# A three-stage attention and mixing kernel: cheaper softmax bookkeeping on VectorE, and the cast of x on ScalarE

## Chip, core and metric

One core of one Trainium2 chip runs the whole program. The metric is the device time of one execution in microseconds. The engines are named as in the profile: PE (TensorE matmul) and PEld (its weight load), DVE (VectorE), ACT (ScalarE), POOL (GpSimd) and SP (SyncE, which issues most of the DMAs).

## The reference, cut to what matters

Three functions follow one another, with batch 4, sequence 576 and model width 512.

```python
# 1: attention over a window of 64 keys, 8 heads of 64
scores = scale * q @ k.T;  scores = where(0 <= rel < 64, scores, -1e9)
attn = exp(scores - max);  attn /= sum(attn) + 1e-09;  x = attn @ v
# 2: four attention experts with a top-2 gate
logits = x @ w_gate;  w = exp(top2 - max);  w /= sum(w) + 1e-09
for e in range(4):                       # causal attention, q, k, v of expert e
    a = exp(scores - max);  a /= sum(a) + 1e-09
    out += [e is among the top 2] * w_e * (a @ v @ wo[e])
# 3: mixing
theta = x @ w_theta;  u = x + w_tok_r @ (x cos theta) + w_tok_i @ (x sin theta)
return u + max(u @ w_ch, 0)
```

## The kernel before, in words

Products that need more than one pass keep each operand as a high part and a low part (`h`, `l`), and `mm3` (L92 to L95) adds three matmuls. `split` (L84 to L90) makes such a pair: a cast for the high part on one engine, and a subtraction for the low part on another.

`phase_a` (L196 on) is function 1: for each of 4 batches and 4 pairs of heads it handles 9 blocks of 64 queries in 3 groups `g` of 3. The scores go to PSUM (L214), L219 masks them and takes the row minimum `nm` of the negated scores, L227 is the Exp with the sums in `sm`, L232 adds 1e-9, L233 takes the reciprocal `rc`, and POOL scales the tile (L234). Transposes (L239), the product with v (L249) and a split into `x0h`, `x0l` follow.

`qk` and `vg_gates` make q, k, v and the gates of function 2. L296 copies v and the logits out of PSUM; L305 to L331 compute the gate weights `gw` for all 576 tokens of a batch. L311 to L317 compare every logit with every other: two copies broadcast them (`lf`, `le`), then a greater-than, an equality, a product with the tie matrix and an addition.

`attn(b, ep)` handles two experts of one batch, in five steps `t` of 64 or 128 queries against the `w` keys up to them. For each expert `i` the scores come in one piece, or for t = 4 in two (`cuts`); L376 masks a piece and takes its minimum, L382 joins the two minima, L384 is the Exp with the sum. L388 adds 1e-9 for both experts, L389 takes the reciprocal, L390 multiplies it by the gate weight, and L392 to L400 scale P, part into `pd` and the rest in place; a table (`KN["SC"]`) says for each pass of `attn` which of these scalings are POOL's (through `pool_mul`, L82) and which are DVE's (L398). A scaling of POOL occurs in 29 of the 40 steps. Transposes (L409, L415), copies to `pT` and the product with v (L424, L428) follow; `wo` projects the result into `x2T`.

Function 3 starts with `x_split(b)`, which splits x in 4 pieces of 128x512 per batch, plus one piece `xt` for each pair of batches (the last 64 tokens of both): casts on DVE (L89, tiles `cx` and `xth`), subtractions on POOL (L90). `theta` makes the angles (L490, L492), sines and cosines on ACT (L493 to L495), products (L508, L517) and their splits (tile `z`). `mix` and `channel` are long runs of matmuls with weights that `load64` takes in from double precision; the last of these loads (`w64k`, `w64c`) are issued from ACT's queue, behind a late Exp of function 2 (L384).

The program's text interleaves these generators by weights (`merge`). The order in each engine's queue is then set when the program is built, by the framework's own simulation of the timeline (`schedule_with_timeline_sim=True` at the end of the file), so it need not be that of the text. Each engine works its queue in order; a wait at its head holds everything behind it.

Of the kernel before, what the change touches and what calls it, by code (L numbers as in the profile page):

```python
# [11 lines left out]
F32 = mybir.dt.float32  # L12
# [5 lines left out]
ALU = mybir.AluOpType  # L18
AX = mybir.AxisListType
PSUM = bass.MemoryType.PSUM  # L20

P = 128
# [35 lines left out]
def kernel(ctx, tc, qT, kT, vw, consts, w_in, w_o, w_th, w_tk, w_ch, outT):  # L58
    nc = tc.nc
# [6 lines left out]
    tie = cst[:, 4 * P :].rearrange("p (a b) -> p a b", a=E)  # L66
# [80 lines left out]


# [36 lines left out]
    def phase_a(b, hps):  # L185
        xh, xl = X[b]
        for hp in hps:
# [10 lines left out]
            for g in range(3):  # L198
# [26 lines left out]
                sm = ap.tile([P, 3], F32, tag="sm", bufs=4, name=f"asm{n}")  # L225
                for i in range(3):
                    nc.scalar.activation(  # L227
                        out=ms[:, i, :], in_=ms[:, i, :], func=AF.Exp,
                        bias=nm[:, i : i + 1], scale=-1.0, accum_out=sm[:, i : i + 1],
                    )  # L230
                rc = ap.tile([P, 3], F32, tag="rc", bufs=4, name=f"arc{n}")
                nc.vector.tensor_scalar_add(out=rc, in0=sm, scalar1=1e-9)  # L232
# [53 lines left out]
    def vg_gates(b):  # L286
# [22 lines left out]
        lf = bp.tile(sh4, F32, tag="glf", name=f"glf{b}")  # L309
        le = bp.tile(sh4, F32, tag="gle", name=f"gle{b}")  # L310
        nc.vector.tensor_copy(out=lf, in_=lg.unsqueeze(2).to_broadcast(sh4))  # L311
        nc.vector.tensor_copy(out=le, in_=lg.unsqueeze(3).to_broadcast(sh4))
        gt = bp.tile(sh4, F32, tag="ggt", name=f"ggt{b}")
        nc.vector.tensor_tensor(out=gt, in0=lf, in1=le, op=ALU.is_gt)
        nc.vector.tensor_tensor(out=le, in0=lf, in1=le, op=ALU.is_equal)
        nc.vector.tensor_mul(out=le, in0=le, in1=tie.unsqueeze(1).to_broadcast(sh4))
        nc.vector.tensor_add(out=gt, in0=gt, in1=le)  # L317
# [26 lines left out]
    def attn(b, ep):  # L344
# [7 lines left out]
        for t in range(5):  # L352
# [4 lines left out]
            if b == B - 1 and ep == 1 and t % 3 == 1:  # L357
                pn = rp.tile([P, 2, S], F32, tag="bmsx", name=f"bms{b}{ep}{t}")
            else:
                pn = bp.tile([P, 2, S], F32, tag="bms", bufs=2, name=f"bms{b}{ep}{t}")  # L360
            sm = bp.tile([P, 2], F32, tag="bsm", bufs=4, name=f"bsm{b}{ep}{t}")
            pd = bp.tile([P, 2, 64], F32, tag="bpd", bufs=2, name=f"bpd{b}{ep}{t}")
            for i in range(2):
# [6 lines left out]
                for ci, (a, z) in enumerate(cuts):  # L370
# [7 lines left out]
                        scale=-0.125, scalar=3.0e38, op0=ALU.add, op1=ALU.min,  # L378
                        accum_out=nm[:m, ci : ci + 1],
                    )  # L380
                if len(cuts) == 2:
                    nc.vector.tensor_tensor(out=nm[:m, 0:1], in0=nm[:m, 0:1],  # L382
                                            in1=nm[:m, 1:2], op=ALU.min)
                ex = nc.scalar.activation(out=ms[:m, :w], in_=ms[:m, :w], func=AF.Exp,  # L384
                                     bias=nm[:m, 0:1], scale=-1.0, accum_out=sm[:m, i : i + 1])
                if (b, ep, t, i) == (3, 1, KN["LT"], 1):
                    late[0] = ex
            nc.vector.tensor_scalar_add(out=sm[:m], in0=sm[:m], scalar1=1e-9)  # L388
            nc.vector.reciprocal(out=sm[:m], in_=sm[:m])  # L389
            nc.vector.tensor_mul(out=sm[:m], in0=sm[:m], in1=gw[:m, t, 2 * ep : 2 * ep + 2])  # L390
            for i in range(2):
                eng = nc.gpsimd if (False, i == 1 and t < 4, i == 1, t >= 2, i == 1 or t >= 3, True)[KN["SC"][2 * b + ep]] else nc.vector  # L392
                ms = pn[:, i]
                for dst, src in ((pd[:m, i], ms[:m, P * t : w]), (ms[:m, : P * t], ms[:m, : P * t])):
                    if src.shape[1] == 0:
                        continue
                    if eng is nc.vector:
                        eng.tensor_scalar_mul(out=dst, in0=src, scalar1=sm[:m, i : i + 1])  # L398
                    else:
                        pool_mul(dst, src, sm[:m, i : i + 1])  # L400
# [55 lines left out]
    def x_split(b):  # L456
        XH[b] = hl_set(xtags, f"cx{b}")
        for c in range(NC):
            split(XH[b][0][c][:, :W4], XH[b][1][c][:, :W4], x2T[b][:, c, :W4], nc.vector, nc.gpsimd)
        if b % 2 == 0:  # L460
# [5 lines left out]
            split(xth, xtl, xt, nc.vector, nc.gpsimd)  # L466
# [256 lines left out]
```

## Time and profile before

| | us |
|---|---|
| median of 3 runs | 546.76 (546.28 to 548.08) |
| the profiled execution: its own time | 546.72 |
| its span in the profile | 544.7 |
| busy in the span: PE, PEld | 518.1 (95%), 483.2 (89%) |
| busy in the span: DVE, ACT, POOL | 357.3 (66%), 323.7 (59%), 298.7 (55%) |

Times in views are counted from the start of the span. The profiled execution's own time is 2.0 us more than its span. Function 1 alone runs until some 58 us; functions 1 and 2 of different batches run side by side until some 320 us, and function 3 begins with its first casts at 276.6 us and runs to the end. Busy shares over the whole span mix stages with different limits, so the views below go by stage. A matmul's end is modelled in this profile: an instruction every 0.13 us is shown as 0.29 us long, so small gaps on PE don't show as idle time.

### The profile page before, as it was taken

The page shows a single profiled execution, that of the slowest core. Times are in us where ns is not written, and L with a number is a line of the kernel's source. Part 1 is how long each engine was busy: PE and PEld are TensorE (multiplying, and loading weights), DVE is VectorE, ACT ScalarE, POOL GpSimd, SP SyncE. Part 2 cuts the span into 40 slices and gives each one's busy share as a digit, 9 for nine tenths or more (in the row PEclk, how much of TensorE's full clock was granted, in tenths as well). Part 3 has the DMA queues.
Part 4 walks back from the last instruction along what each step waited for, and adds up shares of the span by engine and source line. Part 5 has one row for each costly group of instructions (what it writes and reads, how often), then busy time and mean ns, then how long its engine had stood idle before and what let it go on. Part 6 is the DMA issues. An engine that isn't in the chain of part 4 may idle for free.

```text
span 544.7 us, 12460 instructions
## 1 busy us (share of the span) xinstructions
PE 518.1 (95%) x4372; PEld 483.2 (89%) x4372; DVE 357.3 (66%) x1354; ACT 323.7 (59%) x1031; POOL 298.7 (55%) x455
## 2 busy tenths in 40 slices
PE   7879999999999999999799899799999999999997
PEld 5669978898888898989687799699999999999997
DVE  5886898857888688658989868863354435443412
ACT  6967687865868677878577887551344324432410
POOL 5686598635757662237764676962464415641420
PEclk8989999999999999999799899999999999999999
DMA  7654233322224231103003212001000110011002
GB/s 271 203 183 134 67 117 90 92 76 48 98 76 129 93 117 31 40 7 100 32 0 109 88 59 74 6 1 55 34 2 0 43 48 1 1 44 46 0 1 88
DMA packets 20798, 36.80 MB, mean 68 GB/s; under 512 B 2304, under 2 KB 13056, under 8 KB 20736
## 3 DMA queue, kind: packets, MB, share of 16 engines
q1 hardware_dynamic: 19008, 31.55, 18.5%
q10 hardware_dynamic: 1728, 4.46, 2.4%
q8 instruction: 35, 0.57, 0.5%
q14 instruction: 27, 0.22, 0.1%
HBM read 31.28 MB, written 4.72 MB: 66 GB/s over the span
## 4 chain that ended last, share of the span: by engine, by line
PE 69%; DVE 15%; ACT 4%; POOL 4%; DMA 4%; issue 3%; SPq 1%; ACTq 0%; POOLq 0%; DVEq 0%
PE y L94 6%; PE y L93 6%; PE y L95 6%; PE as L214 4%; PE c L94 3%; PE c L95 3%; PE c L93 3%; PE ao L249 3%; PE o L424 3%; PE th L93 3%; PE th L95 3%; PE th L94 3%; PE apt L239 2%; PE bpt L409 2%; PE qk L93 2%
## 5 line engine op out<-in xcount | busy, mean ns | idle before, releaser
L90 POOL TENSOR_TENSOR z<-zf,z 128x256 fp32r<-128x256 f32 x72 | 53.9, 765 | 88.3 <-ACT z L87 88.2
L93 PE MATMUL y<-wkh,z 128*128 128x288 f32 x288 | 86.1, 300 | 0.3 <-DVE x2T L541 0.3
L94 PE MATMUL y<-wkl,z 128*128 128x288 f32 x288 | 85.0, 296 | 0.0
L95 PE MATMUL y<-wkh,z 128*128 128x288 f32 x288 | 84.7, 297 | 0.0
L227 ACT ACTIVATE ams<-ams,anm 128x128 f32<-128x128 f32 x144 | 56.9, 398 | 8.0 <-DVE anm L219 6.5
L93 PEld LDWEIGHTS y<-wkh,z 128*128 128x128 f32 x288 | 54.1, 188 | 0.6 <-DVE x2T L541 0.6
L94 PEld LDWEIGHTS y<-wkl,z 128*128 128x128 f32 x288 | 54.2, 188 | 0.0
L95 PEld LDWEIGHTS y<-wkh,z 128*128 128x128 f32 x288 | 53.9, 188 | 0.0
L493 ACT ACTIVATE ang<-ang 128x256 f32<-128x256 f32 x36 | 14.6, 415 | 65.9 <-DVE ang L492 65.9
L384 ACT ACTIVATE bms<-bms,bnm 64x64 f32<-64x64 f32 (+4 forms) x80 | 44.7, 561 | 14.1 <-DVE bnm L376 7.0
L234 POOL TENSOR_TENSOR ams<-ams,arc 128x384 f32<-128x384 f32 x48 | 40.3, 842 | 23.1 <-DVE arc L233 11.4
L82 POOL TENSOR_SCALAR QD<-qt 64x192 f32<-64x192 f32 x72 | 39.6, 550 | 22.5 <-PE as L214 18.8
L87 ACT CAST z<-zf 128x256 fp32r<-128x256 f32 x72 | 27.3, 403 | 39.1 <-DVE zf L508 14.5
L214 PE MATMUL as<-kt,QD 128*128 128x128 f32 x288 | 45.5, 298 | 3.6 <-ACT QD L209 2.7
L214 PEld LDWEIGHTS as<-kt,QD 128*128 128x128 f32 x288 | 38.4, 203 | 7.8 <-ACT QD L209 3.1
L508 DVE TENSOR_TENSOR zf<-xk,ang 128x256 f32<-128x256 f32 x64 | 25.1, 419 | 28.1 <-ACT ang L495 17.9
L376 DVE CUSTOM_DVE_ANT_0 bms<-bs,mb 128x288 f32<-128x288 f32 (+4 forms) x96 | 38.8, 427 | 5.7 <-PE bs L374 3.1
L219 DVE CUSTOM_DVE_ANT_0 ams<-as,cst 128x128 f32<-128x128 f32 x144 | 34.5, 284 | 7.5 <-PE apt L239 5.0
L93 PE MATMUL th<-wth,cx 128*128 128x256 f32 x128 | 36.6, 287 | 0.5 <-DVE ang L492 0.5
L554 DVE SCALAR_TENSOR_TENSOR x2T<-c,x2T 128x288 f32<-128x288 f32 x32 | 14.5, 457 | 34.0 <-PE c L95 33.8
L94 PE MATMUL th<-wtl,cx 128*128 128x256 f32 x128 | 36.0, 282 | 0.0
L90 POOL TENSOR_TENSOR cu<-x2T,cu 128x288 fp32r<-128x288 f32 x32 | 26.1, 836 | 17.8 <-ACT cu L87 17.8
(196 smaller groups left out, 1752.2 us busy)
## 6 DMA issues: line engine op xcount, KB each, us to landing
vt<-in_dram SPq DMA_DIRECT2D x48, 192.0 KB, 2.4
kt<-in_dram SPq DMA_DIRECT2D x16, 320.0 KB, 3.4
qt<-in_dram SPq DMA_DIRECT2D x16, 288.0 KB, 3.2
out_dram<-x2T SPq DMA_DIRECT2D x32, 144.0 KB, 1.8
w64k<-in_dram SPq DMA_DIRECT2D x5, 576.0 KB, 3.8
w64k<-in_dram ACTq DMA_DIRECT2D x4, 576.0 KB, 3.8
w64t<-in_dram SPq DMA_DIRECT2D x4, 512.0 KB, 4.8
w64c<-in_dram ACTq DMA_DIRECT2D x8, 256.0 KB, 2.8
```

Source lines behind the costliest of these rows:

```text
L82: nc.gpsimd.tensor_scalar(out=out, in0=in_, scalar1=by, scalar2=1.0, op0=ALU.mult, op1=ALU.mult)
L87: nc.scalar.copy(out=dst_h, in_=src)
L90: eng_l.tensor_sub(out=dst_l, in0=src, in1=f32(dst_h))
L93: nc.tensor.matmul(out, wh, xh, start=first, stop=False)
L94: nc.tensor.matmul(out, wh, xl, start=False, stop=False)
L95: nc.tensor.matmul(out, wl, xh, start=False, stop=last)
L214: nc.tensor.matmul(s[:, i, :], QD[g][:, i], kt[:, 64 * blk : 64 * blk + 128], start=True, stop=True)
L219: nc.vector.tensor_tensor_reduce(out=ms[:, i, :], in0=s[:, i, :], in1=ma0 if (g == 0 and i == 0) else ma1, scale=-0.125, scalar=3.0e38, op ...
L227: nc.scalar.activation(out=ms[:, i, :], in_=ms[:, i, :], func=AF.Exp, bias=nm[:, i : i + 1], scale=-1.0, accum_out=sm[:, i : i + 1],)
L234: nc.gpsimd.tensor_mul(out=ms, in0=ms, in1=rc.unsqueeze(2).to_broadcast([P, 3, P]))
L376: nc.vector.tensor_tensor_reduce(out=ms[:m, a:z], in0=s[:m, : z - a], in1=mb[:m, mo + a : mo + z], scale=-0.125, scalar=3.0e38, op0=ALU.ad ...
L384: ex = nc.scalar.activation(out=ms[:m, :w], in_=ms[:m, :w], func=AF.Exp, bias=nm[:m, 0:1], scale=-1.0, accum_out=sm[:m, i : i + 1])
```

## The change

Five edits, and no other line differs.

1. The sums of the Exps go into column 0 of small tiles (`AS`, `BS`) whose column 1 holds 1e-9; 8 memsets write that once at the start, and the tiles are used in turn, four of each kind. In place of the addition of 1e-9 (L232, L388) a `tensor_reduce` adds the two columns.
2. In `x_split` the casts go from DVE to ACT.
3. The multiplication of the reciprocal by the gate weight (L390) is dropped; the scaling of P takes the gate weight as its second per-partition scalar, on DVE and on POOL.
4. The minimum of the first piece is the starting value of the second piece's minimum, and L382 is dropped.
5. In the gates the two copies are dropped: one subtraction of two broadcast views, then two `scalar_tensor_tensor`, for the former six instructions.

```diff
@@ -144,6 +144,17 @@
           tc.alloc_tile_pool(name="xp1", bufs=1, side="left")]
     xbuf = [[xp[i].tile([P, NC, S], F32R, name=f"x{i}{n}") for n in "hl"] for i in range(2)]
     ap = tc.alloc_tile_pool(name="ap", bufs=1, side="right")
+
+    AS = [ap.tile([P, 3, 2], F32, name=f"AS{i}") for i in range(4)]
+    BS = [bp.tile([P, 2, 2], F32, name=f"BS{i}") for i in range(4)]
+    for x in AS + BS:
+        nc.gpsimd.memset(x[:, :, 1], 1e-9)
+    nsum = [0, 0]
+
+    def sums(kind, tiles):
+        nsum[kind] += 1
+        return tiles[nsum[kind] % 4]
+
 
 
     QD = [ap.tile([P, 3, P], F32, name=f"QD{i}") for i in range(3)]
@@ -222,14 +233,14 @@
                         scale=-0.125, scalar=3.0e38, op0=ALU.add, op1=ALU.min,
                         accum_out=nm[:, i : i + 1],
                     )
-                sm = ap.tile([P, 3], F32, tag="sm", bufs=4, name=f"asm{n}")
+                sm = sums(0, AS)
                 for i in range(3):
                     nc.scalar.activation(
                         out=ms[:, i, :], in_=ms[:, i, :], func=AF.Exp,
-                        bias=nm[:, i : i + 1], scale=-1.0, accum_out=sm[:, i : i + 1],
+                        bias=nm[:, i : i + 1], scale=-1.0, accum_out=sm[:, i, 0:1],
                     )
                 rc = ap.tile([P, 3], F32, tag="rc", bufs=4, name=f"arc{n}")
-                nc.vector.tensor_scalar_add(out=rc, in0=sm, scalar1=1e-9)
+                nc.vector.tensor_reduce(out=rc, in_=sm, op=ALU.add, axis=AX.X)
                 nc.vector.reciprocal(out=rc, in_=rc)
                 nc.gpsimd.tensor_mul(
                     out=ms, in0=ms, in1=rc.unsqueeze(2).to_broadcast([P, 3, P])
@@ -306,15 +317,13 @@
         ex = bp.tile([P, 5, E], F32, tag="gex", name=f"gex{b}")
         nc.vector.tensor_sub(out=ex, in0=lg, in1=mx.unsqueeze(2).to_broadcast([P, 5, E]))
         nc.scalar.activation(out=ex, in_=ex, func=AF.Exp)
-        lf = bp.tile(sh4, F32, tag="glf", name=f"glf{b}")
-        le = bp.tile(sh4, F32, tag="gle", name=f"gle{b}")
-        nc.vector.tensor_copy(out=lf, in_=lg.unsqueeze(2).to_broadcast(sh4))
-        nc.vector.tensor_copy(out=le, in_=lg.unsqueeze(3).to_broadcast(sh4))
+        lf, lo = lg.unsqueeze(2).to_broadcast(sh4), lg.unsqueeze(3).to_broadcast(sh4)
+        df = bp.tile(sh4, F32, tag="gle", name=f"gdf{b}")
+        nc.vector.tensor_sub(out=df, in0=lf, in1=lo)
         gt = bp.tile(sh4, F32, tag="ggt", name=f"ggt{b}")
-        nc.vector.tensor_tensor(out=gt, in0=lf, in1=le, op=ALU.is_gt)
-        nc.vector.tensor_tensor(out=le, in0=lf, in1=le, op=ALU.is_equal)
-        nc.vector.tensor_mul(out=le, in0=le, in1=tie.unsqueeze(1).to_broadcast(sh4))
-        nc.vector.tensor_add(out=gt, in0=gt, in1=le)
+        nc.vector.scalar_tensor_tensor(out=gt, in0=df, scalar=0.0, in1=tie.unsqueeze(1).to_broadcast(sh4),
+                                       op0=ALU.is_equal, op1=ALU.mult)
+        nc.vector.scalar_tensor_tensor(out=gt, in0=df, scalar=0.0, in1=gt, op0=ALU.is_gt, op1=ALU.add)
         rk = bp.tile([P, 5, E], F32, tag="grk", name=f"grk{b}")
         nc.vector.tensor_reduce(out=rk, in_=gt, op=ALU.add, axis=AX.X)
         nc.vector.scalar_tensor_tensor(
@@ -358,6 +367,7 @@
                 pn = rp.tile([P, 2, S], F32, tag="bmsx", name=f"bms{b}{ep}{t}")
             else:
                 pn = bp.tile([P, 2, S], F32, tag="bms", bufs=2, name=f"bms{b}{ep}{t}")
+            ss = sums(1, BS)
             sm = bp.tile([P, 2], F32, tag="bsm", bufs=4, name=f"bsm{b}{ep}{t}")
             pd = bp.tile([P, 2, 64], F32, tag="bpd", bufs=2, name=f"bpd{b}{ep}{t}")
             for i in range(2):
@@ -375,29 +385,24 @@
                                      start=False, stop=True)
                     nc.vector.tensor_tensor_reduce(
                         out=ms[:m, a:z], in0=s[:m, : z - a], in1=mb[:m, mo + a : mo + z],
-                        scale=-0.125, scalar=3.0e38, op0=ALU.add, op1=ALU.min,
-                        accum_out=nm[:m, ci : ci + 1],
+                        scale=-0.125, scalar=nm[:m, 0:1] if ci else 3.0e38,
+                        op0=ALU.add, op1=ALU.min, accum_out=nm[:m, ci : ci + 1],
                     )
-                if len(cuts) == 2:
-                    nc.vector.tensor_tensor(out=nm[:m, 0:1], in0=nm[:m, 0:1],
-                                            in1=nm[:m, 1:2], op=ALU.min)
                 ex = nc.scalar.activation(out=ms[:m, :w], in_=ms[:m, :w], func=AF.Exp,
-                                     bias=nm[:m, 0:1], scale=-1.0, accum_out=sm[:m, i : i + 1])
+                                     bias=nm[:m, ci : ci + 1], scale=-1.0, accum_out=ss[:m, i, 0:1])
                 if (b, ep, t, i) == (3, 1, KN["LT"], 1):
                     late[0] = ex
-            nc.vector.tensor_scalar_add(out=sm[:m], in0=sm[:m], scalar1=1e-9)
+            nc.vector.tensor_reduce(out=sm[:m], in_=ss[:m], op=ALU.add, axis=AX.X)
             nc.vector.reciprocal(out=sm[:m], in_=sm[:m])
-            nc.vector.tensor_mul(out=sm[:m], in0=sm[:m], in1=gw[:m, t, 2 * ep : 2 * ep + 2])
             for i in range(2):
                 eng = nc.gpsimd if (False, i == 1 and t < 4, i == 1, t >= 2, i == 1 or t >= 3, True)[KN["SC"][2 * b + ep]] else nc.vector
                 ms = pn[:, i]
                 for dst, src in ((pd[:m, i], ms[:m, P * t : w]), (ms[:m, : P * t], ms[:m, : P * t])):
                     if src.shape[1] == 0:
                         continue
-                    if eng is nc.vector:
-                        eng.tensor_scalar_mul(out=dst, in0=src, scalar1=sm[:m, i : i + 1])
-                    else:
-                        pool_mul(dst, src, sm[:m, i : i + 1])
+                    eng.tensor_scalar(out=dst, in0=src, scalar1=sm[:m, i : i + 1],
+                                      scalar2=gw[:m, t, 2 * ep + i : 2 * ep + i + 1],
+                                      op0=ALU.mult, op1=ALU.mult)
             yield 0.25 * (t + 1)
             pT = bp.tile([P, 5, 2, P], F32, tag="bpT", bufs=2, name=f"bpT{b}{ep}{t}")
             for j0 in range(0, t, 2):
@@ -456,14 +461,14 @@
     def x_split(b):
         XH[b] = hl_set(xtags, f"cx{b}")
         for c in range(NC):
-            split(XH[b][0][c][:, :W4], XH[b][1][c][:, :W4], x2T[b][:, c, :W4], nc.vector, nc.gpsimd)
+            split(XH[b][0][c][:, :W4], XH[b][1][c][:, :W4], x2T[b][:, c, :W4], nc.scalar, nc.gpsimd)
         if b % 2 == 0:
             xt = kp.tile([P, NC, P], F32, tag="xt", name=f"xt{b}")
             for k in range(2):
                 pool_mul(xt[:, :, 64 * k : 64 * k + 64], x2T[b + k][:, :, W4:], 1.0)
             xth = kp.tile([P, NC, P], F32R, tag="xth", name=f"xth{b}")
             xtl = kp.tile([P, NC, P], F32R, tag="xtl", name=f"xtl{b}")
-            split(xth, xtl, xt, nc.vector, nc.gpsimd)
+            split(xth, xtl, xt, nc.scalar, nc.gpsimd)
             XT[0] = xt, xth, xtl
 
     def theta(b, dh):
```

## Rows read from the trace of the kernel before

**Rows 1.** Busy time by engine in stages of the run, with the column line.

```profile
core 0: us, PE busy (x) PEld busy (x) DVE busy (x) ACT busy (x) POOL busy (x), PEclk, DMA share, GB/s
0.00:58.00 58.00, 49.55 (x439) 42.79 (x440) 40.64 (x202) 42.86 (x159) 41.15 (x72) 0.94 0.61 195
58.00:260.00 202.00, 197.63 (x1859) 176.82 (x1857) 160.18 (x740) 151.27 (x529) 118.54 (x214) 1.00 0.26 79
260.00:320.00 60.00, 53.03 (x391) 46.91 (x390) 51.72 (x171) 43.39 (x119) 36.98 (x44) 0.91 0.15 50
320.00:360.00 40.00, 36.41 (x281) 35.41 (x281) 32.65 (x71) 24.30 (x69) 31.10 (x37) 1.00 0.12 41
360.00:540.00 180.00, 180.00 (x1400) 180.00 (x1399) 71.19 (x171) 61.92 (x157) 70.92 (x89) 1.00 0.08 26
```

**Rows 2.** The same columns as rows 1, in four stretches of 5 us.

```profile
260.00:265.00 5.00, 1.45 (x7) 1.16 (x6) 4.87 (x14) 3.25 (x10) 4.67 (x6) 0.78 0.01 6
265.00:270.00 5.00, 4.64 (x18) 4.19 (x17) 4.75 (x20) 3.11 (x7) 2.96 (x6) 0.54 0.00 0
300.00:305.00 5.00, 3.27 (x24) 2.44 (x23) 5.00 (x13) 2.63 (x7) 5.00 (x5) 0.88 0.59 200
345.00:350.00 5.00, 2.31 (x18) 2.11 (x17) 5.00 (x7) 1.06 (x3) 5.00 (x5) 1.00 0.00 0
```

**Rows 3.** Chain that ended last, shares by line: 260 to 280, 280 to 300 us.

```profile
by line: DVE bms L376 11.2%; DVE cx L89 10.3%; DVE gle L315 6.9%; DVE gsm L325 6.6%; PE qk L93 6.5%; DVE KL L282 6.4%; DVE gex L320 5.7%; DVE ggt L317 5.6%; PE qk L94 5.3%; PE qk L95 5.3%; DVE QS L279 4.7%; issue 4.2%; DVE ol L90 2.1%; PE b
...
by line: DVE bms L376 19.4%; issue 8.7%; DVE bsm L388 7.4%; DVE bpT L411 5.2%; DVE ol L90 4.6%; DVE bms L398 4.4%; ACT bms L384 4.4%; DVE bpd L398 4.2%; DVE KL L282 4.1%; PE o L424 4.0%; PE bs L372 4.0%; DVE bnm L382 3.6%; DVE xth L89 3.5%;
```

**Rows 4.** The same chain piece by piece, 340 to 360 us: start, us, what.

```profile
344.88 3.82 DVE cx L89 x3
348.69 0.66 DVE zf L508 x2
```

**Rows 5.** What PE waited for: us in total, times, longest.

```profile
PE xk L486 <- DVE zf L508: 2.7, 1, 2.7
```

**Rows 6.** DVE groups by line and shape: count, busy us, mean ns, idle before.

```profile
L232 DVE TENSOR_SCALAR arc<-asm 128x3 f32<-128x3 f32 x48 | 13.1, 272 | 8.0 <-ACT ams L227 7.6
...
L89 DVE CAST cx<-x2T 128x512 fp32r<-128x512 f32 x16 | 13.0, 846 | 0.1
...
L388 DVE TENSOR_SCALAR bsm<-bsm 128x2 f32<-128x2 f32 x32 | 10.1, 314 | 8.4 <-ACT bms L384 8.2
...
L390 DVE TENSOR_TENSOR bsm<-bsm,gw 128x2 f32<-128x2 f32 x32 | 7.2, 226 | 0.5
...
L382 DVE TENSOR_TENSOR bnm<-bnm 128x1 f32<-128x1 f32 x16 | 4.3, 270 | 0.2
...
L317 DVE TENSOR_TENSOR ggt<-ggt,gle 128x80 f32<-128x80 f32 x4 | 2.8, 690 | 0.1
...
L324 DVE TENSOR_REDUCE gsm<-gex 128x5 f32<-128x20 f32 x4 | 0.7, 171 | 0.1
...
L311 DVE COPY glf<-lg 128x80 f32<-128x80 f32 x4 | 0.9, 223 | 0.0
```

**Rows 7.** Two DVE lines by themselves: shortest/median/longest ns, first and last start.

```profile
L232 DVE TENSOR_SCALAR arc<-asm x48: 141/169/1296, 8.3 to 229.0; 128x3 f32<-128x3 f32 x48
...
L388 DVE TENSOR_SCALAR bsm<-bsm x40: 150/170/921, 61.1 to 305.3; 128x2 f32<-128x2 f32 x32, 64x2 f32<-64x2 f32 x8
```

**Rows 8.** An ACT group of the shape of the casts.

```profile
L130 ACT ACTIVATE wth<-wtut 128x512 fp32r<-128x512 f32 x4 | 2.5, 629 | 0.4 <-POOL wtut L122 0.4
```

**Rows 9.** ACT in order of time, 344 to 350 us.

```profile
349.12 0.71 ACT L87 CAST z<-zf 128x256 fp32r<-128x256 f32 x2 [3.77 <-DVE zf L508]
```

**Rows 10.** POOL groups by line and shape.

```profile
L82 POOL TENSOR_SCALAR bms<-bms,bsm 128x256 f32<-128x256 f32 x11 | 5.3, 487 | 0.6 <-ACT bpT L419 0.6
...
L82 POOL TENSOR_SCALAR xt<-x2T 128x256 f32<-128x256 f32 x4 | 1.6, 407 | 0.0
...
L70 POOL MEMSET halfpi<- 128x1 f32 x1 | 0.1, 99 | 0.0
```

## The prediction

> **What bounds the kernel now.** I read the stages first, since the five edits touch different ones [rows 1]. From 360 to 540 us PE and its weight loads are busy for all of 180 us, while DVE works 71 us: nothing that is taken off DVE there can pay. Before 360 us it is otherwise. PE shows 8.5 us of idle time up to 58 us (58.00 less 49.55), 4.4 us from 58 to 260, 7.0 us from 260 to 320 and 3.6 us from 320 to 360; 23 us in all are the room of this change, and small gaps that the modelled ends hide come on top. DVE is the busiest of the other engines in the last three of these stages, and from 260 to 320 us it has 51.72 of 60 us.
>
> Second, the worst stretches [rows 2]. From 260 to 265 us PE works 1.45 of 5 us and DVE 4.87; in the next 5 us the granted clock is 0.54, near 1.2 of 2.4 GHz, after that stall. From 300 to 305 and from 345 to 350 us DVE and POOL are both full and PE is not. There the queue of DVE sets the pace.
>
> Third, what of the chain in those stretches is a line that the change touches [rows 3]. From 260 to 280 us the casts `cx` take 10.3% of 20 us, 2.1 us, and the gate lines L315 and L317 6.9 and 5.6%, 2.5 us. From 280 to 300 us L388 takes 7.4%, 1.5 us, L382 3.6%, 0.7 us, and the cast of `xth` 3.5%, 0.7 us. Further on three casts hold DVE from 344.88 to 348.69 us, and the products `zf` follow only then [rows 4]; PE waits 2.7 us for them [rows 5].
>
> **The change part by part.** First what DVE is relieved of, in busy time.
>
> *Sums.* L232 takes 0.272 us on average, 48 times, and L388 0.314, 32 times and 8 at half the rows [rows 6]. Alone they would be as quick as their medians, 0.17 us; the longest are 1.30 and 0.92 us [rows 7]. No row shows a reduction of 2 or 3 pairs. The nearest is L324, 20 elements to 5, 0.171 us; its bounds here are 0.14, the shortest addition, and 0.27 to 0.31, the addition's own mean. I take 0.16, for it has fewer elements than L324 and no such stretched one stands in its mean. That is 48 x 0.11 = 5.3 us for L232 and 40 x 0.14 = 5.6 us for L388.
>
> The Trainium skill, "VectorE: DVE Perf Modes", section "Rules for kernel authors", speaks against this edit: it calls `tensor_reduce` the slowest operation of the engine and advises restructuring. By it these 10.9 us would not be won and the sum would be 540.9 instead of 539.2; L324's 0.171 us against L388's 0.314 speaks for the row.
>
> *Products and minima.* L390 goes, 32 x 0.226 us and 8 shorter ones, 8.3 us at most; L382 goes, 4.3 us [rows 6]. In L382's place the second piece of t = 4 waits for the first piece's accumulator. Behind that wait on DVE stand whatever evacuations the order has put there, and PE's next score bank waits for the second piece. Bounds: nothing, and L382's own 0.27 us, 16 times; I take nothing, since the wait is on the instruction directly before.
>
> *Gates.* Six groups, L311 first with 0.9 us and L317 last with 2.8 us, make 10.1 us in four batches [rows 6]. Three remain, of the same 80 elements and two inputs. Bounds for one are L311's 0.22 and L317's 0.69 us; I take 0.5, so 6 us remain and 4 us, 40%, go.
>
> *Casts.* 16 of 0.846 us [rows 6] and two `xth` leave DVE, some 15 us. ACT pays 18 x 0.63 = 11.3 us by L130, an ACT instruction of that shape [rows 8]. Ten of the 18 fall before 360 us, 6.3 us. ACT has 16.6 us free from 260 to 320 (60.00 less 43.39) and 15.7 from 320 to 360 [rows 1]; at the place of the three casts it sits idle for 3.77 us, waiting for DVE [rows 9], and three casts are 1.9 us. So I cost them at nothing; were that idle time filled, the 1.9 us would stand before the casts of `z`. ACT's queue also issues the last loads of weights, and a cast ahead of an issue makes that load 0.63 us later; PE has other matmuls in these stretches, so nothing, and 0.63 us for each where it has none. POOL's subtractions still follow each cast.
>
> The Trainium skill speaks against this edit too: by the cycle tables of "VectorE: DVE Perf Modes", section "The TRN2 errata", a 512-element fp32 copy is an estimated 0.33 us on VectorE and 0.61 on ScalarE. By them the three casts would be 1.0 us, which is all that could be won of the 2.7, and the five before 320 us 1.6 of the 2.8 below, 70% of it let through: the sum would be some 2.5 us less, 541.7. The trace has 0.846 us for a cast on DVE, and the trace decides.
>
> *Scaling.* With two per-partition scalars: no row shows it, on either engine. On POOL a 128x256 scaling by one such scalar takes 0.487 us, by none 0.407 [rows 10]; a second may cost nothing or 0.08 us more. In 29 of the 40 steps POOL scales, so the end is 2.3 us on the path if every step shows it; I take a third, 0.8. On DVE the bounds are nothing and the 0.16 us of L390's quick cases, which would cancel that edit; I take nothing, since the DVE instruction already fetches one scalar.
>
> *Memsets.* Eight at some 0.1 us, by L70 [rows 10], at the start on POOL, and read first by the reduction behind the first Exps, which wait for the loads: nothing; 0.8 us if they stand ahead of what PE waits for.
>
> **The sum**, by what reaches the end. From 320 to 360 us: the wait of 2.7 us [rows 5]. From 260 to 300: casts 2.8, gates 40% of 2.5 = 1.0, L388 1.5 less three reductions of 0.16 = 1.0, L382 0.7, 5.5 us together; what is late next is L376 and the copies to `pT` on the same engine, and PE, so I let 70% through, 3.8 us. From 58 to 260 us DVE saves some 20 us of 160 (three quarters of L388, L390, L382 and the gates, and most of L232), but PE has only 4.4 us of visible idle time; a third, 1.5 us. Up to 58 us L232 alone is touched, beside loads and POOL: 0.3 us. That is 8.3 us, less 0.8 for POOL: 7.5 us. From the profiled execution's 546.72 us this gives 539.2 us; its time stands 0.04 us below the median of the runs, so nothing is added.
>
> **The rivals.**
>
> *More than that.* If DVE no longer lags at the gates, the stall of 260 to 265 us goes whole, and with it the half clock behind it: 3.5 us of idle PE, and up to 2.3 us for the 5 us at 0.54 [rows 2], of which the sum holds some 2, so 3.8 more. With the other 30% of the 5.5 us, 1.7, and no price on POOL, 0.8, it makes 532.9 us. For it: DVE is full there. Against: POOL has 4.67 of those 5 us, and is relieved of nothing.
>
> *The bookkeeping saves nothing*, the change not doing what it says: the reductions stretch as the additions did, or DVE pays for the second scalar what L390 cost. The gain from 260 to 300 us falls by 0.7 to 1.5 us, the one before by 1 us: some 541.5 us. For it: the additions' spread [rows 7], whose cause may lie in their neighbours. Against: L324. The two rules of the Trainium skill named above lead near this case, at 540.9 and 541.7.
>
> *Swallowed.* PE's queue, ACT and POOL, at 43 and 37 of 60 us, are as late as DVE once it is quicker, and only the wait of rows 5 shrinks, by 1 us: 545.7 us. Against: DVE's part of the chain in rows 3.
>
> *Slower: the queues' new order.* The framework writes the order anew from its own costs; that it is not the text's is shown by casts of x at 276 us, ahead of L388 and L382 of attention steps still to come [rows 3]. The mechanism: at the hand-over to the next batch the gate sequence and the subtractions that release q and k stand in one DVE queue, and if the gates stand in front, PE stops. The price is shown at the fourth place, 258 to 270 us: 3.5 us idle and 2.3 us at half clock, some 6 us [rows 2]. The other three such places pay little, for the stage up to 260 has only 4.4 us of idle time in all. One more such place takes 6 of the 7.5 us back; it decides from two on: 539.2 + 12 = 551 us. For it: every edit alters the costs that the order is made from. Against: the three shorter gate instructions lower this price too.
>
> **How the numbers follow.** The forecast, 539.2 us with a range of its own of 535.5 to 543.5, has 0.40; more than that, 0.13; the bookkeeping saving nothing, 0.15; swallowed, 0.13; slower by the order, 0.19. About 0.3%, 1.6 us, is what a measurement of this kernel can tell from no change: faster ends at 545.1, slower begins at 548.4. Faster: 0.40 + 0.13 + 0.15 = 0.68; the same 0.13; slower 0.19. The range reaches down to 531.5, the last microsecond of the first rival left out, and up to 549.5, which takes in the swallowed case and the near end of the slower one.
>
> **What would show it.** Right: reductions of 0.15 to 0.18 us with no long ones; no casts on DVE, and ten on ACT near 0.63 us; `zf` right behind the x2T additions at some 345 us and PE's wait for it gone; DVE busy some 45 us less, ACT some 11 us more. Wrong: the stages up to 260 us longer than before with DVE emptier, which is the order; POOL's scalings above 0.57 us at 128x256; PE waiting for `cx` casts on ACT behind an Exp; or the wait of rows 5 standing as it was.

## The result, and the profile after

The changed kernel takes 540.72 us (median of four runs, 536.14 to 542.42), the one before, timed beside it, 546.52 (four runs, 545.85 to 548.08): 5.8 us less by the medians. The ratio with its 95% interval is 0.9875 [0.9847, 0.9903], 6.8 us less; it is not the quotient of the two medians, and here as in the experiments the two can differ by 1 us. The four runs of the changed kernel lie 6.3 us apart and those of the kernel before 2.2 us, and the profiled execution is the quickest of the four, 536.14 us, 4.6 us under the median. What its rows show beyond these 6 to 7 us belongs to that execution, not to the change.

The page of the kernel after: its span, the busy time of each engine, and the chain that ended last.

```profile
span 534.3 us, 12401 instructions
...
PE 511.4 (96%) x4372; PEld 479.2 (90%) x4372; DVE 326.4 (61%) x1268; ACT 331.2 (62%) x1049; POOL 303.9 (57%) x463
...
PE 76%; ACT 7%; DVE 6%; POOL 4%; DMA 3%; issue 3%; SPq 1%; ACTq 0%; POOLq 0%; DVEq 0%
```

DVE is busy for 30.9 us less than before, ACT for 7.5 and POOL for 5.2 us more. Some five times as much left DVE as left the run.

Busy time by stage of the kernel after, with the columns of [rows 1], and then the four stretches of 5 us of [rows 2], with the ones just ahead, 255 to 260 and 295 to 300 us:

```profile
58.00:260.00 202.00, 195.54 (x1842) 175.78 (x1842) 150.38 (x692) 151.91 (x533) 126.80 (x216) 1.00 0.27 79
260.00:320.00 60.00, 56.07 (x434) 50.71 (x433) 48.48 (x151) 47.99 (x130) 38.70 (x45) 0.94 0.17 58
320.00:360.00 40.00, 40.00 (x315) 39.80 (x315) 26.59 (x67) 26.83 (x75) 32.42 (x41) 1.00 0.09 27
...
255.00:260.00 5.00, 2.80 (x19) 2.31 (x18) 4.70 (x18) 3.41 (x12) 4.60 (x6) 1.00 0.34 115
260.00:265.00 5.00, 3.45 (x14) 2.87 (x13) 4.81 (x17) 1.54 (x4) 3.25 (x5) 0.53 0.02 3
265.00:270.00 5.00, 5.00 (x29) 4.71 (x28) 3.28 (x9) 3.90 (x11) 2.65 (x4) 0.79 0.00 0
...
295.00:300.00 5.00, 3.83 (x32) 3.05 (x32) 4.75 (x15) 4.92 (x13) 3.01 (x3) 1.00 0.52 161
300.00:305.00 5.00, 5.00 (x44) 4.52 (x45) 5.00 (x9) 5.00 (x13) 2.43 (x2) 1.00 0.20 80
345.00:350.00 5.00, 5.00 (x41) 5.00 (x40) 2.03 (x6) 1.35 (x4) 5.00 (x7) 1.00 0.02 3
```

Two of the stretches in which DVE had set the pace are full now, 300 to 305 and 345 to 350 us. Just ahead of the first, though, PE works 3.83 of 5 us from 295 to 300 us, where the kernel before had 4.59: a stall is left there, but the granted clock, 0.88 from 300 to 305 us before [rows 2], stays at 1.00. The stall at the fourth gates is not gone: it begins earlier, with 2.20 us of idle PE from 255 to 260 us and 1.55 in the next 5, and the granted clock falls again, to 0.53 from 260 to 265 us, near 1.2 of 2.4 GHz. Idle time and lost clock together make 3.75 us and (0.47 + 0.21) x 5 = 3.4 us from 255 to 270 us, 7.2 in all; before it was 3.9 us (3.55 and 0.36) and (0.22 + 0.46) x 5 = 3.4, 7.3 in all [rows 2]. This place gave nothing.

From 320 to 360 us PE waits for nothing, where the wait of [rows 5] stood. The place is seen best by two tiles. `y` starts with the first matmul of `mix`, `c` with the first of `channel`; from `c` on every kernel of this study needs 176.1 to 176.3 us to its end, so the distance from `y` to `c` measures that stage by itself. The view of each tile gives the shortest, median and longest ns and the first and last start; the kernel before, then the kernel after:

```profile
L93 PE MATMUL y<-wkh,z x288: 288/295/399, 321.7 to 528.2; 128*128 128x288 f32 x144
L93 PE MATMUL c<-cu,wch x64: 289/296/378, 368.5 to 540.1; 128*128 128x288 f32 x64
```

```profile
L93 PE MATMUL y<-wkh,z x288: 288/295/384, 315.3 to 517.8; 128*128 128x288 f32 x144
L93 PE MATMUL c<-cu,wch x64: 290/295/381, 358.0 to 529.7; 128*128 128x288 f32 x64
```

Before, 368.5 - 321.7 = 46.8 us; after, 358.0 - 315.3 = 42.7 us: 4.1 us of the gain lie here. The other 6.4 us of this profile lie ahead of `y`. The execution is 4.6 us quicker than the median run, and where the runs differ one profile cannot show.

The groups of the kernel after that answer to [rows 6] and [rows 8] (count, busy us, mean ns, idle before):

```profile
L243 DVE TENSOR_REDUCE arc<-AS 128x3 f32<-128x6 f32 x48 | 7.3, 152 | 8.9 <-ACT ams L238 8.6
...
L395 DVE TENSOR_REDUCE bsm<-BS 128x2 f32<-128x4 f32 x32 | 4.8, 151 | 5.3 <-ACT bms L391 5.2
...
L386 DVE CUSTOM_DVE_ANT_0 bms<-bs,mb,bnm 128x288 f32<-128x288 f32 x16 | 8.2, 511 | 1.2 <-PE bs L384 0.8
L386 DVE CUSTOM_DVE_ANT_0 bms<-bs,mb 128x288 f32<-128x288 f32 x16 | 7.1, 447 | 1.3 <-PE bs L384 1.0 <-PE bpt L414 0.2
...
L322 DVE TENSOR_TENSOR gdf<-lg 128x80 f32<-128x80 f32 x4 | 1.7, 432 | 0.0
L326 DVE SCALAR_TENSOR_TENSOR ggt<-gdf,ggt 128x80 f32<-128x80 f32 x4 | 1.5, 383 | 0.0
L324 DVE SCALAR_TENSOR_TENSOR ggt<-gdf,cst 128x80 f32<-128x80 f32 x4 | 1.2, 292 | 0.0
...
L87 ACT CAST cx<-x2T 128x512 fp32r<-128x512 f32 x16 | 9.5, 616 | 9.5 <-PE c L94 9.5
```

The reductions take 0.15 us, the three gate instructions 0.43, 0.29 and 0.38, a cast on ACT 0.616. Of the two pieces of 288 columns at t = 4, the second, which starts from the minimum of the first (`bnm` among its inputs), takes 0.064 us more; in the kernel before, where neither starts from a tile, the 32 of them take 0.448 us on average.

The price of the second scalar, by the view of one line: the kernel before on POOL and on DVE, then the kernel after (shortest, median, longest ns).

```profile
L82 POOL TENSOR_SCALAR bpd<-bms,bsm x47: 311/320/743, 68.1 to 301.4; 128x64 f32<-128x64 f32 x40, 64x64 f32<-64x64 f32 x7
...
L398 DVE TENSOR_SCALAR bpd<-bms,bsm x33: 238/251/1405, 87.2 to 306.8; 128x64 f32<-128x64 f32 x24, 64x64 f32<-64x64 f32 x9
```

```profile
L403 POOL TENSOR_SCALAR bpd<-bms,bsm,gw x47: 386/393/824, 62.9 to 292.7; 128x64 f32<-128x64 f32 x40, 64x64 f32<-64x64 f32 x7
...
L403 DVE TENSOR_SCALAR bpd<-bms,bsm,gw x33: 297/307/1210, 82.8 to 302.7; 128x64 f32<-128x64 f32 x24, 64x64 f32<-64x64 f32 x9
```

By the shortest it is 0.075 us on POOL (386 - 311) and 0.059 on DVE (297 - 238).

### The profile page after: what moved, and what is told of

Read it like the earlier page. It is cut to its first block, busy times and chain, and to the rows that moved or that the text cites. A ratio compares the mean times of both kernels' runs of the same rounds, so it can differ in the third digit from the quotient of the medians.

```text
span 534.3 us, 12401 instructions
## 1 busy us (share of the span) xinstructions
PE 511.4 (96%) x4372; PEld 479.2 (90%) x4372; DVE 326.4 (61%) x1268; ACT 331.2 (62%) x1049; POOL 303.9 (57%) x463
## 4 chain that ended last, share of the span: by engine, by line
PE 76%; ACT 7%; DVE 6%; POOL 4%; DMA 3%; issue 3%; SPq 1%; ACTq 0%; POOLq 0%; DVEq 0%
PE y L95 7%; PE y L94 7%; PE y L93 7%; PE as L225 5%; PE c L94 3%; PE c L93 3%; PE c L95 3%; PE ao L260 3%; PE o L429 3%; PE th L95 3%; PE th L93 3%; PE th L94 3%; PE qk L93 3%; PE bpt L414 2%; PE qk L94 2%
## 5 line engine op out<-in xcount | busy, mean ns | idle before, releaser
L225 PE MATMUL as<-kt,QD 128*128 128x128 f32 x288 | 43.2, 288 | 5.0 <-ACT QD L220 3.6
L225 PEld LDWEIGHTS as<-kt,QD 128*128 128x128 f32 x288 | 36.8, 195 | 8.8 <-ACT QD L220 3.7
L498 ACT ACTIVATE ang<-ang 128x256 f32<-128x256 f32 x36 | 14.5, 416 | 48.4 <-DVE ang L497 48.4
L93 PE MATMUL th<-wth,cx 128*128 128x256 f32 x128 | 36.5, 285 | 1.2 <-DVE ang L497 1.2
L386 DVE CUSTOM_DVE_ANT_0 bms<-bs,mb 64x64 f32<-64x64 f32 (+4 forms) x80 | 32.4, 423 | 6.9 <-PE bs L384 4.8
L95 PE MATMUL th<-wth,cx 128*128 128x256 f32 x128 | 35.6, 284 | 0.0
```

The source lines that it names most:

```text
L93: nc.tensor.matmul(out, wh, xh, start=first, stop=False)
L95: nc.tensor.matmul(out, wl, xh, start=False, stop=last)
L225: nc.tensor.matmul(s[:, i, :], QD[g][:, i], kt[:, 64 * blk : 64 * blk + 128], start=True, stop=True)
L386: nc.vector.tensor_tensor_reduce(out=ms[:m, a:z], in0=s[:m, : z - a], in1=mb[:m, mo + a : mo + z], scale=-0.125, scalar=nm[:m, 0:1] if ci ...
```

## The experiments

Twelve kernels ran, on three chips, each beside runs of the kernel before; their medians there were 546.4, 547.0 and 546.5 us. Ratios are to that kernel, with the 95% interval, and the gains in us are worked out from the ratios. Every one computes the whole of the reference.

### Edit 1 alone: the sums

```diff
-                nc.vector.tensor_scalar_add(out=rc, in0=sm, scalar1=1e-9)
+                nc.vector.tensor_reduce(out=rc, in_=sm, op=ALU.add, axis=AX.X)
...
-            nc.vector.tensor_scalar_add(out=sm[:m], in0=sm[:m], scalar1=1e-9)
+            nc.vector.tensor_reduce(out=sm[:m], in_=ss[:m], op=ALU.add, axis=AX.X)
```

> Only edit 1 (the column of 1e-9 and the reductions), made to the kernel before; every queue keeps the order of before. Theory (work off DVE where DVE is late): the 88 additions become reductions of 0.15 us with none above 0.2, DVE busy falls by some 10 us from 357, the stage from 260 to 300 us and the one before give 2 us: 544.5 us, ratio 0.996. Rival (the gain of the whole change is its new order): the order is the same here, so the ratio stays within 0.3% of 1.

Measured: 546.21 us, 0.9988 [0.9969, 1.0007]. The queues keep the order of the kernel before, so this is the edit and nothing else. The two lines by themselves, and PE's wait for `zf`:

```profile
L244 DVE TENSOR_REDUCE arc<-AS x48: 130/150/160, 8.0 to 228.3; 128x3 f32<-128x6 f32 x48
...
L401 DVE TENSOR_REDUCE bsm<-BS x40: 128/152/160, 61.1 to 304.1; 128x2 f32<-128x4 f32 x32, 64x2 f32<-64x4 f32 x8
...
PE xk L499 <- DVE zf L521: 2.7, 1, 2.7
```

The saving on DVE is there: no reduction is longer than 0.160 us, where the additions reached 1.30 [rows 7], and DVE is busy for 347.6 us, 9.7 less. At the end 0.65 us of it is left, with bounds of -0.4 and 1.7 us. The theory's 2 us did not come; the ratio is the rival's.

### Edit 2 alone: the casts

```diff
-            split(XH[b][0][c][:, :W4], XH[b][1][c][:, :W4], x2T[b][:, c, :W4], nc.vector, nc.gpsimd)
+            split(XH[b][0][c][:, :W4], XH[b][1][c][:, :W4], x2T[b][:, c, :W4], nc.scalar, nc.gpsimd)
...
-            split(xth, xtl, xt, nc.vector, nc.gpsimd)
+            split(xth, xtl, xt, nc.scalar, nc.gpsimd)
```

> Only edit 2 (the casts of x on ACT). Theory: the casts take 0.62 us on ACT, PE's wait of 2.7 us for zf at some 348 us goes, the five casts before 320 us give some 2 us more: 542 us, ratio 0.992. Rival (ACT becomes late in its place): the wait of PE stays above 2 us with ACT as its source, and the ratio is within 0.3% of 1.

Measured: 543.99 us, 0.994 [0.9917, 0.9963], so 3.3 us (2.4 by the medians). Its stage from 320 us, the two tiles, and a wait of PE that is 0.5 us long in the kernel before:

```profile
320.00:360.00 40.00, 39.93 (x314) 39.50 (x313) 28.86 (x70) 29.38 (x83) 31.52 (x39) 1.00 0.13 41
...
L93 PE MATMUL y<-wkh,z x288: 288/295/382, 322.8 to 525.0; 128*128 128x288 f32 x144
L93 PE MATMUL c<-cu,wch x64: 288/296/378, 365.3 to 537.0; 128*128 128x288 f32 x64
...
PE th L93 <- DVE ang L492: 1.4, 1, 1.4
```

From `y` to `c` it is 42.5 us, 4.3 less than before; `y` itself starts 1.1 us later. So the casts pay in the stage where PE had waited for them, and its wait for `zf` is gone. The five casts ahead of 320 us, whose time on DVE went as well, bring nothing in this order, where the theory had some 2 us: PE waits 0.9 us longer for the angles, also DVE's.

### Edit 3 alone: the scaling

```diff
-            nc.vector.tensor_mul(out=sm[:m], in0=sm[:m], in1=gw[:m, t, 2 * ep : 2 * ep + 2])
...
-                        eng.tensor_scalar_mul(out=dst, in0=src, scalar1=sm[:m, i : i + 1])
...
+                    eng.tensor_scalar(out=dst, in0=src, scalar1=sm[:m, i : i + 1],
+                                      scalar2=gw[:m, t, 2 * ep + i : 2 * ep + i + 1],
...
```

> Only edit 3 (the gate weight as second scalar of the scaling). Theory (the second scalar is paid for): each of 87 scalings on POOL takes 0.075 us more and each of 57 on DVE 0.06 us more, 6.5 and 3.4 us, against 8.5 us of DVE for L390; the time moves by no more than the 3 us that another order was seen to move it, 543.5 to 549.5 us. Rival (the product was on the path, as the forecast had it): 1 to 2 us faster, 545 us, with the stage from 260 to 300 us shorter.

Measured: 543.0 us, 0.993 [0.9912, 0.9948], 3.8 us less, though DVE is busy for only 3.9 us less and POOL for 8.3 more. That is just below the theory's range and more than the rival's 1 to 2 us. The three stretches at the fourth gates, and the wait for `zf`:

```profile
255.00:260.00 5.00, 3.04 (x23) 2.57 (x22) 4.84 (x17) 3.27 (x9) 4.57 (x8) 1.00 0.39 120
260.00:265.00 5.00, 4.54 (x28) 3.90 (x29) 4.84 (x18) 4.35 (x12) 4.75 (x6) 1.00 0.02 3
265.00:270.00 5.00, 4.81 (x31) 3.93 (x30) 4.83 (x15) 2.64 (x8) 4.47 (x5) 1.00 0.00 0
...
PE xk L484 <- DVE zf L506: 2.7, 1, 2.7
```

PE is idle here for 1.96 + 0.46 + 0.19 = 2.6 us, and the granted clock stays at 1.00, where it was 0.78 and 0.54 [rows 2]: of the 7.3 us that the place cost before, 4.7 are gone, and `y` starts 5.0 us earlier (316.7 us). That is as much as the whole gain; from `y` to `c` the kernel then takes 48.4 us, 1.6 more than before, at a granted clock of 0.96 from 320 to 360 us. But PE is ahead of the kernel before already at 240 us (2132 matmuls begun, against 2106), the edit does not touch the gates, and the queues' order is a new one too, so the gain cannot be put down to the edit.

### Edits 4 and 5 alone: the minima and the gates

```diff
-                        scale=-0.125, scalar=3.0e38, op0=ALU.add, op1=ALU.min,
+                        scale=-0.125, scalar=nm[:m, 0:1] if ci else 3.0e38,
...
-        nc.vector.tensor_tensor(out=gt, in0=lf, in1=le, op=ALU.is_gt)
...
+        nc.vector.tensor_sub(out=df, in0=lf, in1=lo)
...
```

> Only edits 4 and 5 (chained minima, gate comparisons without copies). Theory: the three gate instructions take some 0.4 us each, 5 us in all for 10, and L382's 4.3 us go, less 1 us for the second pieces' own scalar; the stall behind the fourth gates gets shorter by 1 to 2 us: 545 us, ratio 0.997. Rival (the order decides): 549 us or more, or 543 or less, with the difference in stages where no gates run.

Measured: 550.54 us, 1.006 [1.0047, 1.0073]: slower by 3.3 us with less work on DVE (353.8 us busy). From the row maximum of the logits to the copy of the gate weights it is 4.5, 4.9, 5.0 and 8.6 us in the four batches, against 6.9, 6.9, 6.1 and 11.2 before, and still the run is longer, as the rival had it. PE's longest wait in the stretch from 250 to 275 us, and DVE in order of time just before it ends:

```profile
PE qk L93 <- DVE QS L279: 2.6, 1, 2.6
...
257.44 1.70 DVE L119 TENSOR_SCALAR wtuk<-wtuk 128x576 uint32<-128x576 uint32 x1 [0.70 <-ACT wtuk L117]
259.17 1.05 DVE L120 SCALAR_TENSOR_TENSOR wtuk<-w64k,wtuk 128x576 uint32<-128x576 uint32 x1
260.25 0.46 DVE L279 TENSOR_TENSOR QS<-qk,QS 64x288 fp32r<-64x288 f32 x1
```

Two steps of the loading of weights, 1.70 and 1.05 us, stand in DVE's queue ahead of the subtraction that releases q, at a place where PE was full before (255 to 260 us in the kernel before: 5.00 of 5). No edit is about these steps; they stand there because the order was made anew.

### The order alone

To price that, three kernels change one weight by which the program's text interleaves its generators, and nothing else: the same instructions in another order, twice on the kernel before and once on the kernel after. The line is long and cut here to the weight.

```diff
-    'AT': [12.51,
+    'AT': [15.0,
```

> The kernel before with the same instructions in another order: one weight of the interleaving, AT[0], is 15.0 instead of 12.51, nothing else. Theory: an order by chance moves the time by no more than 0.5%, 544 to 549 us. Rival (the order decides): the time moves by 5 us or more, down or up.

Measured: 550.91 us, 1.0062 [1.004, 1.0085]. Its longest wait of PE is one that the kernel before does not have:

```profile
PE bpt L409 <- DVE ol L90: 3.4, 1, 3.4
```

The second, on the kernel before:

```diff
-    'QK': [16.78, 11.97,
+    'QK': [16.78, 9.5,
```

> As n1_order by another weight, QK[1] 9.5 instead of 11.97. Theory: 544 to 549 us. Rival (the order decides): 5 us or more away from 546.5, and another value than n1_order.

Measured: 549.78 us, 1.0054 [1.0032, 1.0077]. Both times lie above the theory's range and short of the rival's 5 us. The third makes the first edit on the kernel after:

> The changed kernel with the same instructions in another order: AT[0] is 15.0 instead of 12.51, nothing else. Theory (an order by chance is worth up to 4 us either way): 537 to 545 us, and not within 0.3% of 540.7. Rival (the gain stands whatever the order): 539 to 542.5 us.

Measured: 537.93 us, 0.9835 [0.9811, 0.9859], 0.4% under the change itself, with overlapping intervals. So the order of the same work moves this kernel by some 3 us in either variant of before, and perhaps by 2 us on the kernel after. That is as much as each of edits 2, 3 and 4 with 5 moved the total alone. The start of `y` in the three, in the same sequence:

```profile
L93 PE MATMUL y<-wkh,z x288: 288/295/442, 324.8 to 533.5; 128*128 128x288 f32 x144
L93 PE MATMUL y<-wkh,z x288: 288/295/442, 324.5 to 532.7; 128*128 128x288 f32 x144
L93 PE MATMUL y<-wkh,z x288: 288/294/384, 316.5 to 519.7; 128*128 128x288 f32 x144
```

In the three orders of the work of before `y` starts at 321.7, 324.8 and 324.5 us, in the two of the work of after at 315.3 and 316.5 us. The groups lie 5.2 us apart and are 3.1 and 1.2 us wide, so the gain ahead of `y` in these profiles is more than the order alone has moved. The profile of the third order is its median run.

### The change without one edit

Each of these undoes one part of the change, so its diff is that part's, reversed. Without the sums:

> The changed kernel without edit 1: the 88 additions of 1e-9 are back; the queues of PE, ACT and POOL keep the order of the changed kernel but for the 8 memsets. Theory (edit 1 alone gave 0.65 us of 546, since where DVE is late the additions were rarely stretched): the additions cost 10 us of DVE again, and the time is 541 to 542.5 us. Rival (in the quicker whole, the sums are on the path): 544 us or more.

Measured: 538.76 us, 0.9857 [0.984, 0.9873]; every queue keeps the order of the kernel after but for the memsets, and DVE is busy for 335.4 us, 9.0 more. Neither theory nor rival came: 9 us more work on DVE make it no slower. Without the scaling:

> The changed kernel without edit 3: L390's multiplication is back, the scalings take one scalar. Theory (edit 3 gives nothing): within 3 us of the changed kernel, 538 to 544 us; POOL's scaling to bpd has its shortest at 0.31 us again. Rival (edit 3 is worth 2 us as its part of the whole): 543 us or more.

Measured: 540.76 us, 0.9882 [0.9863, 0.9901]. Without the minima and the gates:

> The changed kernel without edits 4 and 5, which alone made the kernel before 3.3 us slower. Theory (that loss is one of order, a stall moved ahead of the fourth gates): here the gates take 2 us longer each time and the order is new again, within 4 us of the changed kernel, 537 to 545 us, and where it differs is a stage without gates. Rival (the edits themselves cost time): 536 to 538 us, with the stages around the gates shorter.

Measured: 536.44 us, 0.9816 [0.9798, 0.9834]. None of the three is measurably slower than the whole change. What edit 3 brought alone is not in the whole; edits 4 and 5 make the whole no quicker, and without them it runs 0.6% quicker, with intervals that do not meet. That is the rival's time, and its sign is there too: PE is idle for 3.0 us from 250 to 275 us at a clock of 1.00, against 4.4 at 0.86 in the kernel after. But the order is a new one here as well, and an order alone moved as much. The whole without edit 2 was not run.

### A fourth use of the column

The gates have an addition of 1e-9 too, L334 of the kernel after, on 5 elements. At the fourth gates it takes 1.43 us there. DVE and then POOL of the kernel after, in order of time:

```profile
261.32 1.43 DVE L334 TENSOR_SCALAR gsm<-gsm 128x5 f32<-128x5 f32 x1
```

```profile
261.31 1.41 POOL L128 TENSOR_TENSOR wkl<-wtuk,wkh 128x576 fp32r<-128x576 f32 x1
```

It begins and ends with the POOL instruction beside it. Two kernels give the gates the column as well, the second of them without edit 3:

```diff
-        ex = bp.tile([P, 5, E], F32, tag="gex", name=f"gex{b}")
+        ex5 = bp.tile([P, 5, E + 1], F32, tag="gex", name=f"gex{b}")
+        nc.gpsimd.memset(ex5[:, :, E], 1e-9)
+        ex = ex5[:, :, :E]
...
-        nc.vector.tensor_reduce(out=sm, in_=ex, op=ALU.add, axis=AX.X)
-        nc.vector.tensor_scalar_add(out=sm, in0=sm, scalar1=1e-9)
+        nc.vector.tensor_reduce(out=sm, in_=ex5, op=ALU.add, axis=AX.X)
```

> The changed kernel with the column of 1e-9 in the gates too: their sum takes five columns, and the addition of 1e-9 behind it is gone. Theory (what POOL stretches at the hand-over of the batches holds PE): the addition took 0.59 us on average and 1.43 us in the fourth gates; without it the stall of PE there gets shorter by about 1 us: 539.7 us against 540.7. Rival (something else is late there by as much): no difference beyond 0.3%.

Measured: 537.81 us, 0.9823 [0.9804, 0.9843], 0.5% under the kernel after, 2.8 us where the theory had 1.

> The changed kernel without edit 3 and with the column of 1e-9 in the gates (u3_no_scale and i1_gate_sum in one). Theory (edit 3 is worth nothing by its work, the gates' addition some 1 to 3 us): 537 to 540 us. Rival (both were accidents of the order): 541 us or more.

Measured: 533.99 us, 0.9773 [0.9759, 0.9787], 1.1% under the kernel without edit 3 and the quickest kernel of the study; it beats the kernel before by 12.4 us and the kernel after by 1.0%. Both settings point the same way. But the place of the theory does not show it: idle time of PE and lost clock from 250 to 275 us make 7.4 us with the column for 7.9 in the kernel after, and 5.9 for 6.8 without edit 3, so 0.5 and 0.9 us of gains of 2.8 and 6.0. The order is a new one in both, and that the column in the gates pays is not shown.

## Why the prediction was right, and where it was not

**The total.** The forecast was 7.5 us less; 5.8 came by the medians and 6.8 by the ratio, within its own range. That it came so near is in part luck: by the profiles its largest term was too large and the next two too small. Nor does the number alone tell the forecast, 539.2 us, from the rival at 541.5.

**From 320 to 360 us**, forecast 2.7 us by the wait of [rows 5]. Right in mechanism and place, and the term was too small: 4.3 us in edit 2 alone, 4.1 in the whole. The distance from `y` to `c` is 42.5 to 43.5 us in all eight kernels with the casts on ACT and 46.8 to 49.0 in all six without, under whatever order, and PE's wait for `zf` is 2.7 us in all these six and at most 0.8 in the eight, so this is shown of the casts alone. Five of these six had a granted clock of 0.96 from 320 to 360 us; the sixth, the kernel before, had 1.00 [rows 1], and against it the difference is 4.1 in the whole and 4.3 in edit 2 alone. The wait counts only the gap that the modelled ends leave visible: the kernel before has 3.6 us of idle PE in this stage [rows 1], which is nearer. That three casts fit into ACT's idle time at no cost held: they stand at 337.69 to 339.69 us, ahead of the casts of `z`, and nothing waits.

ACT of the kernel after in order of time, at that place:

```profile
337.69 1.13 ACT L87 CAST cx<-x2T 128x512 fp32r<-128x512 f32 x2
338.74 0.43 ACT L87 CAST cu<-x2T 128x288 fp32r<-128x288 f32 x1
339.07 0.62 ACT L87 CAST cx<-x2T 128x512 fp32r<-128x512 f32 x1
339.59 0.71 ACT L87 CAST z<-zf 128x256 fp32r<-128x256 f32 x2
```

**From 260 to 300 us**, forecast 3.8 us: 70% of 5.5 us of DVE's part of the chain, half of it the casts'. This is the step that failed: the term was too large. Singly, the casts there brought nothing, the sums 0.65 us over the whole run, and the minima and gates made it slower. In the whole, PE's work can be followed, for every kernel begins the same 2698 matmuls ahead of `y`. Where three quarters of the columns that these move are begun, at 244.7 us in the kernel before, the kernel after is some 4.7 us ahead, and at `y` 6.4; the third order is ahead by 2.4 and 5.2. From there to `y` these two gain 1.7 and 2.8 us, and the five kernels without an edit or with the column in the gates 1.1 to 3.7. A share of the chain that ended last says what stood on that chain, not what the run loses when it goes: in the kernel after PE waits from 245 to 325 us for `QS` (1.5 us), the angles (1.2) and `KL` (1.0), all still DVE's.

**From 58 to 260 us**, forecast 1.5 us, and up to 58 us 0.3. By the same count this was too little: 4.7 us in the profile of the kernel after, of which 1.7 are the granted clock up to 58 us (0.97, before 0.94), 2.4 in the third order, 1.5 to 4.2 in the other five. Which edit gave it is not shown; edit 1 alone, with the order kept and 9.7 us less on DVE, is 0.7 us ahead there. In the median run of the whole less is left: some 1.7 us, 5.8 less the 4.1 from `y` to `c`, or 2.7 by the ratio, for all that lies ahead of `y`, if its runs are alike from there on, which one profile cannot show.

**What DVE is relieved of**, forecast 45 us, measured 30.9. The forecast's own parts add up to 42.5 (10.9, 8.3, 4.3, 4 and 15). The durations of the removed work were right: reductions 0.152 and 0.151 us for 0.16, gates under 0.5 each, casts gone. Two prices taken at nothing were not nothing. The second scalar on DVE costs 0.059 us in each of 57 scalings, 3.4 us, and the groups of L403 on DVE are 5.7 us above those of L398 with what stretches among them; the chained minimum costs 0.064 us sixteen times, 1.0 us, of the 4.3 that L382 took. Added up over all groups, DVE's work fell from 414.4 to 377.2 us, by 37.2; the instructions overlap at their ends, so the busy time fell by less.

**POOL's second scalar**, forecast 0 to 0.08 us: 0.075 by the shortest `bpd`, the upper bound, and 0.069 by the mean at 128x256 (0.556 us for 0.487). A third of 2.3 us on the path was charged for it; the kernel without edit 3 is level with the whole, so its gain and its cost balance there to within the intervals.

**The rivals.** *More than that* did not come: the stall at the fourth gates stayed. *The bookkeeping saves nothing* is wrong in the mechanism of its sums, for no reduction stretched, and half right in that of its scaling, where 3.4 us of the 8.5 of L390 came back; at the end the sums are worth nothing that can be measured. The Trainium skill, "VectorE: DVE Perf Modes", section "Rules for kernel authors", calls `tensor_reduce` the slowest operation of the engine; on the 4 to 6 elements here the trace does not bear that out, 0.15 us against a mean of 0.27 to 0.31 and a median of 0.17 for the addition that it replaced. *Swallowed* did not come: the wait of [rows 5] went whole, not by 1 us, and `y` starts earlier as well. *The queues' new order* is real: edits 4 and 5 alone were slower at the place that the prediction named, though it was the loading of weights, not the gates, that stood ahead of q, and unchanged work in another order moved by 0.5 to 0.6%. The price was some 3 us, where 6 for a place and 12 for two had been reckoned. In the whole it did not win over the casts.

**What stays open.** The four single gains are 0.65, 3.3, 3.8 and -3.3 us, 4.5 together against 6.8 for the whole by its ratio, or 3.1 against 5.8 by the medians, and all but the first come with an order of their own. Edit 2 has a place that tells it from the order. Edit 1 was measured twice with the order kept, 0.65 us alone and -1.0 in the whole, neither of which can be told from nothing. What edits 3, 4 and 5 are worth apart from the order, between -4 and +4 us, these runs do not tell; nor which of them gives the lead ahead of `y`, nor why the runs of the kernel after spread over 6.3 us. In the kernel with the third order the two runs at a mean clock of 1.00 take 536.0 and 536.2 us and the three below it 537.9 to 538.8, so there the clock seems to be part of it; in the kernel after it does not suffice, for at 0.99 stand both 536.14 and 541.86 us.

## What to carry to other kernels

Count on what an engine is relieved of only where another engine's wait ends on it: the casts before `zf` gave all of their wait and more, and with 31 us taken off DVE in all the run became only 6 to 7 us shorter. Where a framework writes the order anew, run the same work in two or three other orders first: here they differ by 0.6%, and an edit that brings less cannot be credited from one timing. Replacing tiny additions by reductions over a column that holds the constant took 9 to 10 us off DVE and nothing that could be measured off the run; whether it pays on the chain before a stall, as in the gates, is not shown.

## What was not expected of the hardware

The reductions did not stretch: 88 of them after and 88 in the first experiment, none over 0.161 us, though 61 and 53 of them ran beside a POOL instruction. Of the 88 additions before, 27 took over 0.25 us, and an addition on 5 elements takes 1.43 us beside a POOL instruction of 1.41. The Trainium skill, "SBUF — State Buffer", section "SBUF: two separate sides", says that VectorE in a two-port mode, or with two inputs from SBUF, and GpSimd hold a shared pair of ports by an exclusive lock for a whole instruction. The trace agrees in that the addition ends with POOL's instruction (262.75 and 262.72 us); that the reductions did not wait for it is read from their 176 durations.

A second per-partition scalar is not free on either engine, 0.075 us on POOL and 0.059 on DVE, and a starting value read from a tile costs the fused minimum 0.064 us. And a stall can cost about as much again by the granted clock as by the idle time: 3.4 us beside 3.9 at the fourth gates before, 3.4 beside 3.75 after. But it cost nothing beside 2.6 with edit 3 alone, nor beside 4.8 us of idle time from 250 to 275 us in the kernel without the sums, whose queues are in the order of the kernel after; what makes the difference these runs do not show.
